# A hand-ordered attention and maxout-FFN kernel: a new order of the pieces behind the first 62, with its PSUM banks and drains, and four softmax products on VectorE

## The chip, the core and the metric

The kernel runs on one core of one Trainium2 chip, alone. The time is the device time of one execution in microseconds (us): the median of three executions of the kernel before is 164.94 us (164.56 to 165.78).

## What is computed

Eight batches of eight heads, 576 positions, head size 64. Each head's keys and values are first gathered into 32 memory slots with the softmax of `phi`; then every query attends to the 32 slots; the result goes through an FFN whose hidden layer is the largest of three products.

```python
a = softmax(phi, over positions)                    # (b, h, s, m), m = 32
k_m = einsum('bhsm,bhsd->bhmd', a, k)
v_m = einsum('bhsm,bhsd->bhmd', a, v)
attn = softmax(q @ k_m.T / 8, over the 32 slots)
x = (attn @ v_m) as (4608 tokens, 512)
h = maximum(maximum(x @ w1, x @ w2), x @ w3)        # 768 wide
out = h @ w_out                                     # 512 wide, float32
```

All inputs are float32 in HBM; the loads turn them into bfloat16 on the way (`phi` stays float32).

## The kernel before

The whole kernel is straight-line code. Every batch is cut into pieces, and one long list of words, written out by hand, says in which order the pieces are emitted: `F8@2` is piece F8 of batch 2. Each engine carries out its own instructions in the order in which they were emitted; across engines only semaphores hold them to data and to buffers. So the list is at once the order of TensorE (PE), of VectorE (DVE), of ScalarE (ACT), of GpSimd (POOL) and of POOL's loads.

The letters:

- `L0` to `L3` start a load on POOL's queue: phi, k, v and q of a batch, 576 KB each as it lands. `H`, `Y` are the loads of batch 0 and of the weights. A load has to wait, with POOL behind it, until the buffer that it fills has been read: phi and q have two buffers each, k and v of even and of odd batches one each (`kvo0`, `kvo1`).
- `E`: ACT takes the exponential of phi (L229). `r0`, `r1`: POOL packs k, then v, of a batch into one tile, `kvr` (L103). `B`: PE multiplies them, 72 small products (L249); it needs both packs. `N`: DVE normalises. `K`: PE transposes, a drain follows.
- `Q0`, `Q1`: DVE transposes the two halves of q (L313). `S`: PE's scores (L333), and ACT's exponential of them (L342).
- `a`, `s`, `c`, `m`, `X` with 0 or 1: the softmax over the 32 slots for one half of the heads: DVE transposes (L387), sums (L395), takes the reciprocal (L404); POOL multiplies (`m`, L409); DVE transposes back into `attn` (L417). There are 14 of each.
- `D0` to `D3`: the slots' values are folded into the weights (PE L440, then a drain to `wp`). `F0` to `F11`: the FFN's first layer for a batch, 4 matmuls each (L466). An even F is drained by a ReLU (L170 on ACT), an odd F by a maximum on DVE (L479), which writes `hT`.
- `T0` to `T4`: the second layer for 128 tokens: 6 matmuls with `wo_sb` and `hT` (L497), 2 with `wp3` and `attn` (L506; 4 at L515 for T4), a drain to `ot` (L172), and a store on SP's queue. `T` of a batch needs all its `hT`.

PSUM's eight banks are handed out by a second list, one digit a use; B, S, D and F take the bank named and the next one. A piece on PE waits until the last reader of its banks is done. Which of ACT and DVE drains a piece is in `EVAC`; a `!` behind a word turns it round for that piece:

```python
EVAC = {"D": "avaaa", "T": "vavav", "K": "v", "W": "vvv", "O": "aaaa", "F": "aaaaaa"}
if (EVAC[kind][n] == "a") != swap:
```

So T0, T2 and T4 are drained by DVE without a mark and by ACT with one; T1 and T3 the other way round.

Of the kernel before, what the change touches and what calls it, by code (L numbers as in the profile page):

```python
# [15 lines left out]
def kernel(  # L16
# [68 lines left out]
    def load_ph(b):  # L85
        ph = inp.tile([P, NP, NC, M], FP32, name="ph")
        loaded.setdefault(b, {})["ph"] = ph
        dst = ph.rearrange("p j c m -> p j (c m)")
        if b == 0:
            for h in halves:  # L90
                nc.sync.dma_start(out=dst[:, h], in_=by_pair(phi, b)[:, h])
        else:
# [8 lines left out]

    def pack(b, i):
        nc.gpsimd.tensor_copy(  # L103
            out=kvrs[b % 2][:, :, :, D * i : D * (i + 1)], in_=kvos[b % 2][:, 1 - i]
        )
# [132 lines left out]
    def att_kv(b, part=None):  # L238
        s = st[b]
        kvp = two_banks()  # L240
        s["kvp", part] = kvp
        kv = loaded[b]["kv"]
        nd = {None: 2 * D + 1, 0: 2 * D, 1: D}[part]
        kvr = kvrs[b % 2]
        for c in range(NC):
            for j in range(NP):
                for a in range(NG):
                    r = slice(HP * a, HP * (a + 1))
                    nc.tensor.matmul(  # L249
                        kvp[M * j : M * (j + 1), a, 0:nd],  # L250
                        lhsT=s["e"][r, j, c, :],
                        rhs={
                            None: lambda: kvr[r, j, c, 0:nd],
                            0: lambda: k_and_ones(kv, r, j, c),
                            1: lambda: kv[r, 0, j, c, :],
                        }[part](),
                        start=(c == 0),
                        stop=(c == NC - 1),
                        tile_position=(HP * a, M * j),
                    )  # L260
# [331 lines left out]


    for w in """
        E@0 H2@0 H0@0 L3@0 Z25@0 B0@0 Y2@0 I@0 N0@0 Z2@0 K0@0! Q0@0 Q1@0 Z9@0 S@0 Z2@0 M0@0 M1@0
        R0@0 R1@0 W0@0 Y3@0 W1@0 W2@0 Z6@0 O1@0 H3@0 O3@0 O2@0 H1@0 X1@0 B1@0 X0@0 N1@0
        K1@0 O0@0 Y0@0 D1@0! D0@0! D3@0 F8@0 F10@0 F2@0 V0@0 F6@0 F0@0! Y1@0 D2@0 D4@0 F4@0
        L0@1 V1@0 F1@0 E@1 F3@0 L1@1 F5@0 F9@0 F7@0 L3@1 F11@0 B0@1 T3@0 N0@1 K0@1! L2@1 Q1@1
        L2@2 L1@2 Q0@1 L0@2 V2@0 T0@0! L3@2 S@1 T1@0 a0@1 s0@1 c0@1 m0@1 B1@1 N1@1 a1@1 L1@3
        K1@1 s1@1 D0@1 D1@1! D2@1 c1@1 m1@1 X0@1 L3@3 r1@2 X1@1 T2@0! L2@3 F6@1 F10@1 F7@1 F2@1  # L600
        F3@1 F4@1 F0@1 r0@2 E@2 F5@1 F1@1 F11@1 L0@3 L0@4 F8@1 L2@4 F9@1 B@2 D3@1 N@2 Q1@2
        T0@1! K@2 T2@1! r0@3 Q0@2 S@2 a0@2 a1@2 s1@2 c1@2 m1@2 T4@1! D1@2! s0@2 D2@2 c0@2 m0@2
        X1@2 D0@2 T3@1 Q0@3 L3@4 X0@2 Q1@3 T1@1 F0@2 F4@2 F8@2 F6@2 F9@2 E@3 F7@2 r1@3 F5@2
        F10@2 F1@2 B@3 L1@4 D3@2 N@3 L0@5 F2@2 F11@2 E@4 F3@2 L1@5 K@3 r1@4 L2@5 T2@2! S@3 T3@2
        a0@3 s0@3 c0@3 m0@3 D0@3 D2@3 a1@3 s1@3 c1@3 X0@3 D1@3! Q0@4 m1@3 T1@2 L3@5 L2@6 T0@2!
        X1@3 F10@3 r0@4 F2@3 F4@3 E@5 Q1@4 r0@5 F5@3 F3@3 L1@6 F8@3 B@4 N@4 D3@3 F9@3 F6@3
        F11@3 L0@6 K@4 F0@3 F7@3 F1@3 S@4 a0@4 T4@3! s0@4 a1@4 D0@4 c0@4 s1@4 r1@5 c1@4 D3@4
        m0@4 X0@4 Q0@5 T0@3! D1@4! D2@4 B@5 T3@3 m1@4 X1@4 L0@7 F10@4 Q1@5 N@5 F8@4 K@5 F6@4
        F9@4 S@5 F7@4 L3@6 F2@4 F4@4 a0@5 L1@7 a1@5 F0@4 s0@5 r1@6 F3@4 D0@5 r0@6 s1@5 c1@5 E@6
        D3@5 m1@5 c0@5 F1@4 T1@3 L2@7 F11@4 L3@7 E@7 F5@4 m0@5 B@6 D1@5! D2@5 X1@5 N@6 T2@3!  # L610
        X0@5 F6@5 F8@5 Q0@6 Q1@6 K@6 F4@5 F9@5 S@6 F7@5 r0@7 a0@6 F2@5 a1@6 s0@6 c0@6 F0@5
        F10@5 m0@6 F1@5 s1@6 c1@6 F11@5 F5@5 T0@4! F3@5 X0@6 T2@4! r1@7 D0@6 D1@6! Q0@7 B@7
        m1@6 N@7 X1@6 T2@5! K@7 T3@4 Q1@7 S@7 a0@7 F2@6 s0@7 a1@7 s1@7 c1@7 m1@7 c0@7 F4@6
        T4@5! D3@6 D2@7 D0@7! T0@5! D3@7 D2@6 X1@7 m0@7 D1@7! T1@4 X0@7 F6@7 F3@6 T1@5 F4@7
        F8@7 F0@7 F5@6 F10@6 F7@7 F9@7 F10@7 F5@7 F0@6 F11@7 F6@6 F1@7 F7@6 F2@7 F8@6 F11@6
        F9@6 F1@6 F3@7 T0@6! T0@7! T3@5 T2@7! T2@6! T1@6 T1@7 T3@6 T4@7! T3@7
    """.split():
# [32 lines left out]
```

## Time and profile before

| | before |
|---|---|
| median of three executions (lowest to highest) | 164.94 us (164.56 to 165.78) |
| profiled execution: span from first to last instruction | 163.3 us |
| mean granted PE clock in it | 0.995 |
| POOL's load queue: packets, share of the 16 DMA engines' span | 16080, 68.7% |
| store queue of SP: packets, share | 5728, 17.2% |
| HBM read, written | 39.32 MB, 9.44 MB |
| PE waits in the profile from 46 to 115 us (over 0.15 us) | none |

The span is that of one execution under the profiler; the median is 1.6 us above it. A busy PE in the profile may still wait a little between matmuls, since their ends are modelled; its real pace is read from the starts of equal matmuls.

The trace also has the moment at which each load had landed. The loads behind the weights land one after the other in the order in which they were issued; k3 is the k of batch 3, ph4 the phi of batch 4:

| place | before: load | issued, us | landed, us |
|---|---|---|---|
| 1 to 4 | ph1, k1, q1, v1 | 9.4 to 19.9 | 32.2, 34.8, 37.7, 40.5 |
| 5 to 8 | v2, k2, ph2, q2 | 24.7 to 31.2 | 44.1, 48.5, 50.0, 53.5 |
| 9 to 11 | k3, q3, v3 | 43.5, 45.6, 48.4 | 56.3, 59.1, 63.5 |
| 12, 13 | ph3, ph4 | 51.2, 51.9 | 65.6, 67.2 |
| 14 | v4 | 52.7 | 71.3 |
| 15 | q4 | 62.3 | 74.2 |
| 16 to 19 | k4, ph5, k5, v5 | 65.6 to 73.4 | 77.3, 79.2, 83.0, 87.3 |
| 20 to 23 | q5, v6, k6, ph6 | 77.6 to 85.9 | 89.8, 94.0, 98.0, 100.1 |
| 24 to 28 | ph7, q6, k7, v7, q7 | 91.7 to 102.9 | 102.0, 104.7, 108.3, 111.8, 114.6 |

Stores of 256 KB run beside them: 18 land between 44.1 and 112.4 us.

### The profile page before, as it was taken

The page shows a single profiled execution, that of the slowest core. Times are in us where ns is not written, and L with a number is a line of the kernel's source. Part 1 is how long each engine was busy: PE and PEld are TensorE (multiplying, and loading weights), DVE is VectorE, ACT ScalarE, POOL GpSimd, SP SyncE. Part 2 cuts the span into 40 slices and gives each one's busy share as a digit, 9 for nine tenths or more (in the row PEclk, how much of TensorE's full clock was granted, in tenths as well). Part 3 has the DMA queues.
Part 4 walks back from the last instruction along what each step waited for, and adds up shares of the span by engine and source line. Part 5 has one row for each costly group of instructions (what it writes and reads, how often), then busy time and mean ns, then how long its engine had stood idle before and what let it go on. Part 6 is the DMA issues. An engine that isn't in the chain of part 4 may idle for free.

```text
span 163.3 us, 4838 instructions
## 1 busy us (share of the span) xinstructions
PE 153.8 (94%) x2080; PEld 85.3 (52%) x2080; DVE 90.4 (55%) x181; ACT 100.6 (62%) x151; POOL 69.5 (43%) x71
## 2 busy tenths in 40 slices
PE   7978798899899999999999999999999999999990
PEld 2433444564377436743673575576553468744450
DVE  2023704798838665849399748879749128810010
ACT  4205445845497488778885899994658976223320
POOL 7932205100599259657968957646403100000000
PEclk9999999999999999999999999999999999999998
DMA  6999999999999999999999999996313130014333
GB/s 150 152 206 207 205 210 217 274 208 210 253 313 238 209 253 379 274 210 293 252 263 206 232 355 264 191 233 150 130 69 129 69 128 0 0 68 186 135 128 130
DMA packets 21974, 31.77 MB, mean 195 GB/s; under 512 B 1216, under 2 KB 16576, under 8 KB 21952
## 3 DMA queue, kind: packets, MB, share of 16 engines
q0 software_dynamic: 16080, 21.43, 68.7%
q1 hardware_dynamic: 5728, 9.90, 17.2%
q8 instruction: 16, 0.26, 0.6%
q10 hardware_dynamic: 144, 0.13, 0.2%
q14 instruction: 6, 0.05, 0.1%
HBM read 39.32 MB, written 9.44 MB: 299 GB/s over the span
## 4 chain that ended last, share of the span: by engine, by line
PE 83%; DMA 9%; POOL 2%; ACT 2%; issue 1%; DVE 1%; ACTq 0%; POOLq 0%
PE psum L497 29%; PE psum L466 28%; DMA wo_sb<-in_moe_w_out_dram 9%; PE psum L506 8%; PE psum L440 6%; PE psum L249 4%; PE psum L192 3%; PE psum L333 2%; PE psum L515 1%; ACT h L170 1%; PE psum L538 1%; PE psum L298 1%; POOL kvo L97 1%; ACT wp L172 1%; POOL qq L110 0%
## 5 line engine op out<-in xcount | busy, mean ns | idle before, releaser
L497 PE MATMUL psum<-wo_sb,hT 128*128 128x512 bf16 x210 | 51.3, 380 | 0.0
L466 PE MATMUL psum<-attn,wp 128*128 128x288 bf16 x384 | 50.5, 286 | 0.1
L479 DVE TENSOR_TENSOR hT<-psum,h 128x576 bf16<-128x576 f32 x48 | 34.2, 749 | 18.0 <-PE psum L466 12.5
L466 PEld LDWEIGHTS <-wp 128*128 128x128 bf16 x384 | 36.7, 98 | 13.2 <-issue 2.0
L172 ACT COPY ot<-psum 128x512 f32<-128x512 f32 x35 | 20.7, 591 | 32.1 <-PE psum L506 25.2
L497 PEld LDWEIGHTS <-hT 128*128 128x128 bf16 x210 | 19.2, 97 | 24.0 <-issue 4.3
L172 ACT CAST wp<-psum 128x1024 bf16<-128x1024 f32 (+1 forms) x31 | 29.2, 995 | 3.8 <-PE psum L440 2.0
L103 POOL COPY kvr<-kvo 128x2304 bf16<-128x2304 bf16 x12 | 25.3, 2111 | 13.7 <-DMA kvo<-in_k_dram 10.1
L170 ACT ACTIVATE h<-psum 128x576 bf16<-128x576 f32 x47 | 28.4, 659 | 3.5 <-PE psum L466 3.3
L409 POOL TENSOR_TENSOR t<-t,sm 128x576 bf16<-128x576 bf16 x14 | 16.1, 1154 | 24.6 <-DVE sm L404 24.4
L506 PE MATMUL psum<-wp,attn 128*128 128x512 bf16 x62 | 18.4, 379 | 0.0
L159 PE MATMUL psum<-warm 128*128 128x512 bf16 x44 | 12.1, 427 | 1.2 <-DVE warm L128 1.2
L313 DVE STREAM_TRANSPOSE qT<-qq 128x576 f32<-128x576 f32 x16 | 11.7, 747 | 1.4 <-DMA qq<-in_q_dram 1.4
L342 ACT ACTIVATE e<-psum 128x576 bf16<-128x576 f32 x16 | 9.6, 652 | 3.8 <-PE psum L333 3.8
L229 ACT ACTIVATE e<-ph 128x1152 bf16<-128x1152 f32 (+1 forms) x9 | 9.6, 1065 | 1.7 <-DMA ph<-in_phi_dram 1.6
L395 DVE TENSOR_REDUCE sm<-t 128x18 f32<-128x576 bf16 x14 | 10.3, 738 | 0.2
L387 DVE STREAM_TRANSPOSE t<-e 128x288 f32<-128x288 f32 x14 | 6.4, 465 | 6.2 <-ACT e L342 6.1
L97 POOL DMA_DIRECT2D kvo<-in_v_dram x9 | 6.7, 749 | 7.1 <-PE psum L249 4.1
L506 PEld LDWEIGHTS <-attn 128*128 128x128 bf16 x62 | 6.1, 98 | 7.1
L110 POOL DMA_DIRECT2D qq<-in_q_dram x8 | 6.2, 770 | 6.6 <-DVE h L174 3.7
L555 DVE COPY ot<-psum 128x256 f32<-128x256 f32 x1 | 0.4, 425 | 15.4 <-PE psum L546 15.4
L249 PEld LDWEIGHTS <-e 64*32 64x32 bf16 x720 | 6.9, 90 | 3.7 <-issue 3.3
(57 smaller groups left out, 114.4 us busy)
## 6 DMA issues: line engine op xcount, KB each, us to landing
out_dram<-ot SPq DMA_DIRECT2D x35, 256.0 KB, 5.6
qq<-in_q_dram POOLq DMA_DIRECT2D x8, 576.0 KB, 12.2
ph<-in_phi_dram POOLq DMA_DIRECT2D x7, 576.0 KB, 14.4
kvo<-in_k_dram POOLq DMA_DIRECT2D x7, 576.0 KB, 14.6
kvo<-in_v_dram POOLq DMA_DIRECT2D x7, 576.0 KB, 15.6
w_sb<-in_moe_w_dram POOLq DMA_DIRECT2D x3, 768.0 KB, 19.0
wo_sb<-in_moe_w_out_dram POOLq DMA_DIRECT2D x1, 768.0 KB, 14.6
ph<-in_phi_dram SPq DMA_DIRECT2D x2, 288.0 KB, 3.0
```

Of the source, the lines that this page charges most:

```text
L103: nc.gpsimd.tensor_copy(out=kvrs[b % 2][:, :, :, D * i : D * (i + 1)], in_=kvos[b % 2][:, 1 - i])
L159: nc.tensor.matmul(po[:, 0:BANK], lhsT=warm[:, 0:P], rhs=warm, start=True, stop=True)
L170: nc.scalar.activation(out=out_, in_=in_, func=AF.Relu)
L172: nc.scalar.copy(out=out_, in_=in_)
L249: nc.tensor.matmul(kvp[M * j : M * (j + 1), a, 0:nd], lhsT=s["e"][r, j, c, :], rhs={None: lambda: kvr[r, j, c, 0:nd], 0: lambda: k_and_one ...
L313: nc.vector.transpose(out=s["qT"][:, j].rearrange("p j c r e -> p (j c r e)").bitcast(FP32), in_=loaded[b]["q"][:, j].rearrange("p j c d - ...
L395: nc.vector.tensor_reduce(out=sm, in_=s["t", g].rearrange("p n r e -> p n e r"), op=ALU.add, axis=mybir.AxisListType.X,)
L409: nc.gpsimd.tensor_tensor(out=t, in0=t, in1=s["sm", g].unsqueeze(2).to_broadcast([P, S // HP, R, 2]), op=ALU.mult,)
L466: nc.tensor.matmul(acc[:, h, 0:SH], lhsT=wps[b][:, g, w * DF + ft * P : w * DF + (ft + 1) * P], rhs=attn[:, g, c0 : c0 + SH], start=(g == ...
L479: nc.vector.tensor_tensor(out=hT[:, ft, (b % 2) * S : (b % 2 + 1) * S].rearrange("p (h n) -> p h n", h=2), in0=a, in1=s["h1", ft], op=ALU.max,
L497: nc.tensor.matmul(po, lhsT=hT[:, fc, c0 : c0 + P], rhs=wo_sb[:, fc, :], start=(n == 0), stop=False,)
L506: nc.tensor.matmul(po, lhsT=attn[:, g, c0 : c0 + P], rhs=wp3s[b][:, g, :], start=False, stop=(g == NG - 1),)
```

## The change

The first 62 words of the order stay as they are. Behind them all words are the same in kind and number, 368 in all, and stand in another order; the bank list is new from its fourth digit on; the marks `!` sit on other words (33 before, 42 after). `m` takes a mark now, and four have one: `m1@1`, `m1@2`, `m0@2` and `m0@5` run on DVE. `r` could take one (ACT would pack), and none has it.

By kind, the drains that change hands: six ReLUs of F (128x576) go from ACT to DVE, twelve drains of T (128x512) and three of D (128x1024) go from ACT to DVE, and four drains of K (128x384) go from DVE to ACT.

```diff
-    def pack(b, i):
-        nc.gpsimd.tensor_copy(
-            out=kvrs[b % 2][:, :, :, D * i : D * (i + 1)], in_=kvos[b % 2][:, 1 - i]
-        )
+    def pack(b, i, swap):
+        out_, in_ = kvrs[b % 2][:, :, :, D * i : D * (i + 1)], kvos[b % 2][:, 1 - i]
+        if swap:
+            nc.scalar.copy(out=out_, in_=in_)
+        else:
+            nc.gpsimd.tensor_copy(out=out_, in_=in_)
...
-            00224460026701101401264026402640264026452063420643064206420642064562074206742064
...
+            00232204420145545045024602460460246024674620540246206246024604260160272046740624
...
-    def att_mul(b, g):
+    def att_mul(b, g, swap):
         s = st[b]
         t = s["t", g]
-        nc.gpsimd.tensor_tensor(
+        (nc.vector if swap else nc.gpsimd).tensor_tensor(
...
-        L0@1 V1@0 F1@0 E@1 F3@0 L1@1 F5@0 F9@0 F7@0 L3@1 F11@0 B0@1 T3@0 N0@1 K0@1! L2@1 Q1@1
-        L2@2 L1@2 Q0@1 L0@2 V2@0 T0@0! L3@2 S@1 T1@0 a0@1 s0@1 c0@1 m0@1 B1@1 N1@1 a1@1 L1@3
-        K1@1 s1@1 D0@1 D1@1! D2@1 c1@1 m1@1 X0@1 L3@3 r1@2 X1@1 T2@0! L2@3 F6@1 F10@1 F7@1 F2@1
-        F3@1 F4@1 F0@1 r0@2 E@2 F5@1 F1@1 F11@1 L0@3 L0@4 F8@1 L2@4 F9@1 B@2 D3@1 N@2 Q1@2
-        T0@1! K@2 T2@1! r0@3 Q0@2 S@2 a0@2 a1@2 s1@2 c1@2 m1@2 T4@1! D1@2! s0@2 D2@2 c0@2 m0@2
-        X1@2 D0@2 T3@1 Q0@3 L3@4 X0@2 Q1@3 T1@1 F0@2 F4@2 F8@2 F6@2 F9@2 E@3 F7@2 r1@3 F5@2
-        F10@2 F1@2 B@3 L1@4 D3@2 N@3 L0@5 F2@2 F11@2 E@4 F3@2 L1@5 K@3 r1@4 L2@5 T2@2! S@3 T3@2
-        a0@3 s0@3 c0@3 m0@3 D0@3 D2@3 a1@3 s1@3 c1@3 X0@3 D1@3! Q0@4 m1@3 T1@2 L3@5 L2@6 T0@2!
-        X1@3 F10@3 r0@4 F2@3 F4@3 E@5 Q1@4 r0@5 F5@3 F3@3 L1@6 F8@3 B@4 N@4 D3@3 F9@3 F6@3
...
+        D2@0 D4@0 F4@0 L0@1 V1@0 F1@0 E@1 F3@0 L1@1 F5@0 F9@0 F7@0 L3@1 F11@0 B0@1 N0@1
+        Q0@1 Q1@1 V2@0 T3@0 K0@1! T0@0 S@1 L2@1 a0@1 B1@1 L0@2 s0@1 N1@1 c0@1 T1@0 L1@2
+        L2@2 a1@1 K1@1 D0@1 s1@1 c1@1 m0@1 X0@1 m1@1! D1@1! X1@1 D2@1! T2@0! F0@1 F6@1!
+        L0@3 F2@1 F10@1! L3@2 F3@1 r0@2 E@2 F8@1 F7@1 F11@1 F4@1 F1@1 F9@1 L2@3 F5@1
+        D3@1 r1@2 B@2 E@3 N@2 T0@1! K@2! Q0@2 Q1@2 T2@1 S@2 T1@1 D1@2! D0@2 a0@2 D3@2
+        L1@3 a1@2 s0@2 T3@1 T4@1! L2@4 L3@3 s1@2 c1@2 r1@3 L0@4 D2@2 m1@2! X1@2 r0@3
+        c0@2 B@3 L1@4 m0@2! L1@5 X0@2 N@3 L3@4 F0@2 r1@4 F4@2 F8@2 F2@2 L0@5 L2@5 r0@4
+        Q0@3 Q1@3 F5@2 F1@2 L1@6 F6@2 E@4 F3@2 F9@2 F10@2 L3@5 F7@2 F11@2 K@3 T2@2 S@3
+        a0@3 B@4 s0@3 D3@3 c0@3 m0@3 a1@3 T1@2 s1@3 N@4 c1@3 X0@3 T3@2 m1@3 D1@3 X1@3
+        D0@3 Q1@4 D2@3 L0@6 T0@2! F6@3 Q0@4 F4@3 r0@5 F8@3 F5@3 E@5 L2@6 F9@3 F2@3 F7@3
...
```

The banks of the pieces that the prediction walks through, in the new list: B@3 0, F0@2 6, F4@2 2, F8@2 4, F2@2 6, F5@2 0, F1@2 2, F6@2 4, F3@2 6, F9@2 0, F10@2 4, F7@2 2, F11@2 6.

More of the change, by code (lines that the diff above doesn't have):

```diff
@@ L140 @@
             """
-            00224460026701101401264026402640264026452063420643064206420642064562074206742064
-            20642064201640264102640264026402640264072406247026402640264024602406520462046204
-            62704267402640264124602416420642064206420642067676767670
+            00232204420145545045024602460460246024674620540246206246024604260160272046740624
+            60246042601624067042602604260426042604267260430626024062402602640246240264034602
+            42046201624042614620460426426420640460424026062467676764
             """.split()
@@ L569, in issue @@
             "H": lambda: load_kv(b, i % 2, halves[i // 2]),
-            "r": lambda: pack(b, i),
+            "r": lambda: pack(b, i, swap),
             "E": lambda: [att_exp(b, h) for h in (halves if b == 0 else [slice(0, NP)])],
@@ L579, in issue @@
             "c": lambda: att_rec(b, i),
-            "m": lambda: att_mul(b, i),
+            "m": lambda: att_mul(b, i, swap),
             "X": lambda: (ones_mul if (b, i) in ONES else att_back)(b, i),
@@ L594 @@
     for w in """
-        E@0 H2@0 H0@0 L3@0 Z25@0 B0@0 Y2@0 I@0 N0@0 Z2@0 K0@0! Q0@0 Q1@0 Z9@0 S@0 Z2@0 M0@0 M1@0
-        R0@0 R1@0 W0@0 Y3@0 W1@0 W2@0 Z6@0 O1@0 H3@0 O3@0 O2@0 H1@0 X1@0 B1@0 X0@0 N1@0
-        K1@0 O0@0 Y0@0 D1@0! D0@0! D3@0 F8@0 F10@0 F2@0 V0@0 F6@0 F0@0! Y1@0 D2@0 D4@0 F4@0
-        L0@1 V1@0 F1@0 E@1 F3@0 L1@1 F5@0 F9@0 F7@0 L3@1 F11@0 B0@1 T3@0 N0@1 K0@1! L2@1 Q1@1
-        L2@2 L1@2 Q0@1 L0@2 V2@0 T0@0! L3@2 S@1 T1@0 a0@1 s0@1 c0@1 m0@1 B1@1 N1@1 a1@1 L1@3
-        K1@1 s1@1 D0@1 D1@1! D2@1 c1@1 m1@1 X0@1 L3@3 r1@2 X1@1 T2@0! L2@3 F6@1 F10@1 F7@1 F2@1
@@ L607 @@
[L607 to L616, printed above, removed]
+        E@0 H2@0 H0@0 L3@0 Z25@0 B0@0 Y2@0 I@0 N0@0 Z2@0 K0@0! Q0@0 Q1@0 Z9@0 S@0 Z2@0
+        M0@0 M1@0 R0@0 R1@0 W0@0 Y3@0 W1@0 W2@0 Z6@0 O1@0 H3@0 O3@0 O2@0 H1@0 X1@0 B1@0
@@ new lines @@
+        X0@0 N1@0 K1@0 O0@0 Y0@0 D1@0! D0@0! D3@0 F8@0 F10@0 F2@0 V0@0 F6@0 F0@0! Y1@0
+        D2@0 D4@0 F4@0 L0@1 V1@0 F1@0 E@1 F3@0 L1@1 F5@0 F9@0 F7@0 L3@1 F11@0 B0@1 N0@1
[3 more added lines that the diff above has]
+        D3@1 r1@2 B@2 E@3 N@2 T0@1! K@2! Q0@2 Q1@2 T2@1 S@2 T1@1 D1@2! D0@2 a0@2 D3@2
@@ new lines @@
+        L1@3 a1@2 s0@2 T3@1 T4@1! L2@4 L3@3 s1@2 c1@2 r1@3 L0@4 D2@2 m1@2! X1@2 r0@3
[3 more added lines that the diff above has]
+        D0@3 Q1@4 D2@3 L0@6 T0@2! F6@3 Q0@4 F4@3 r0@5 F8@3 F5@3 E@5 L2@6 F9@3 F2@3 F7@3
+        F10@3 r1@5 F3@3 K@4! F0@3 L3@6 F11@3 S@4 F1@3 B@5 a0@4 N@5 D2@4 L1@7 D3@4 s0@4
@@ new lines @@
+        c0@4 T3@3 K@5! Q1@5 a1@4 s1@4 c1@4 T1@3! m0@4 D0@4 D1@4! Q0@5 m1@4 X0@4 X1@4
+        D2@5 T4@3 S@5 a0@5 L0@7 a1@5 r1@6 T2@3! s0@5 F6@4! F2@4 F0@4 F4@4 s1@5 F1@4 F3@4
+        F10@4 L2@7 F7@4 F8@4 L3@7 F11@4 c0@5 r0@6 c1@5 E@6 F9@4 T0@3! F5@4 m1@5 D1@5!
+        D0@5 B@6 m0@5! X1@5 X0@5 N@6 Q0@6 T3@4 F4@5 F10@5! F0@5 F11@5 F8@5 K@6 r0@7 Q1@6
+        F9@5 F5@5 F1@5 T0@4 E@7 r1@7 S@6 B@7 D3@5 a0@6 T2@4! a1@6 N@7 Q0@7 F6@5 F2@5!
+        D1@6! D3@6 F3@5 Q1@7 s1@6 c1@6 K@7! T1@4 F7@5 s0@6 S@7 c0@6 T3@5! D2@7! a1@7
@@ L617 @@
+        a0@7 m1@6 m0@6 X0@6 s0@7 c0@7 X1@6 m0@7 D2@6 D0@6 T4@5! D3@7 D1@7 D0@7 s1@7 c1@7
+        T0@5! F10@6 F2@6 F3@6 X0@7 m1@7 F6@6 X1@7 F11@6 F4@6 T1@5 F0@6 F10@7 F4@7! F1@6
+        F8@6 F7@6 F11@7 T2@5! F2@7 F5@6 F9@6 F8@7 T3@6 F3@7 F0@7 F5@7 F9@7 T1@6! F6@7
+        F1@7 F7@7 T2@6 T0@7 T4@7! T1@7! T2@7! T0@6 T3@7
     """.split():
```

## The prediction

> **What bounds the kernel now.** I first read the page's busy times and slices, then the busy time by stage.
>
> ```profile
> PE 153.8 (94%) x2080; PEld 85.3 (52%) x2080; DVE 90.4 (55%) x181; ACT 100.6 (62%) x151; POOL 69.5 (43%) x71
> ...
> DMA  6999999999999999999999999996313130014333
> ```
>
> ```profile
> core 0: us, PE busy (x) PEld busy (x) DVE busy (x) ACT busy (x) POOL busy (x), PEclk, DMA share, GB/s
> ...
> 46.00:68.00 22.00, 22.00 (x300) 13.31 (x299) 14.24 (x28) 17.39 (x26) 15.77 (x14) 1.00 1.15 277
> 68.00:115.00 47.00, 46.98 (x766) 27.48 (x743) 36.26 (x78) 37.51 (x54) 33.25 (x28) 1.00 1.11 239
> ```
>
> PE has no idle time from 46 to 115 us, so there a new order can win hardly anything. The second thing to see is that the loads are just as full: the DMA digits are 9 up to 110 us, and by the table of landings one load ends as the next begins, from 26 to 114.6 us. The n-th load lands at a time set by the loads ahead of it, whenever it was issued. So there are two clocks, PE's work and the queue of loads, and the old order fits them together. The question is whether the new one still does. POOL's timeline and the chain of waits show the fit:
>
> ```profile
> 56.34 2.11 POOL L103 COPY kvr<-kvo 128x2304 bf16<-128x2304 bf16 x1 [2.90 <-DMA kvo<-in_k_dram]
> ...
> 63.51 2.11 POOL L103 COPY kvr<-kvo 128x2304 bf16<-128x2304 bf16 x1 [0.39 <-DMA kvo<-in_v_dram]
> ...
> 71.38 2.11 POOL L103 COPY kvr<-kvo 128x2304 bf16<-128x2304 bf16 x1 [2.30 <-DMA kvo<-in_v_dram]
> ```
>
> ```profile
> 63.39 4.41 PE psum L466 x36
> 67.80 0.73 PE psum L249 x68
> ...
> 77.11 1.29 PE psum L497 x6
> 78.41 0.43 PE psum L506 x2
> ...
> 81.78 0.73 PE psum L249 x71
> ```
>
> POOL packs as soon as k or v is there (56.3, 63.5, 71.4 us), so it is already waiting for loads; PE runs B@3 at 67.80, 2.2 us after its last pack, and B@4 at 81.78. The chain gives the prices: an F 4.41/9 = 0.49, B 0.73, a T 1.29 + 0.43 = 1.73.
>
> **The order of PE against the loads.** I count pieces. The old order has PE at 67.80 when it begins B@3. In the new order the work ahead of F9@2 is the same set with B@3, D3@2 (0.22), F2@2 and F3@2 more and F10, F7 and F9@2 less: 0.73 + 0.22 + 0.98 - 1.47 = +0.46. Unhindered, PE comes to F9@2 at 68.26. B@4 follows after F9, F10, F7, F11 (1.96), K@3 (0.17), T2@2 (1.73) and S@3 (0.42), at 72.5. In the old order twelve further pieces, 8.8 us of them (three T, three D, six F), stood ahead of B@4. So the new order wants batch 4 nine us earlier, and the loads cannot give it.
>
> Landing of q3. In the new order the loads behind the weights are ph1 k1 q1 v1, ph2 k2 v2, ph3 q2 v3 k3, v4 q3 ph4, k4. The first fourteen are the same fourteen loads as in the old order, where the last of them landed at 71.3 (the third POOL row). ph4 is now last and takes 67.2 - 65.6 = 1.6; q3, the thirteenth, lands at 69.6. In the old order it landed at 59.1. The store traffic can shift this: ph4, the old thirteenth, landed at 67.2, and v4 in its place costs 1.2 more (2.8 for a lone k, v or q), so 68.4 is the early end.
>
> Who waits. Q0@3 and Q1@3 stand on DVE ahead of the maximum of F5@2, and a DVE that waits for q3 lets nothing pass. DVE has finished N@3 by about 66.3 (B@3 at 64.5, then 0.73 and 1.05 of L269 to L283). So it stands idle until 69.65, transposes twice (0.74 each, 0.70 apart), and ends the maximum of F5@2 (0.75) at 71.80. PE meanwhile gets through F1, F6 and F3 (their banks come free from ACT or earlier work), but F9@2 takes bank 0, F5's. It starts at 71.86: 3.60 late.
>
> Landing of k4. It is fifteenth, and the first fifteen are again the same set, whose last landed at 74.2. POOL's pack takes 2.11, so B@4 starts at 74.2 + 0.05 + 2.11 + 0.06 = 76.4 at the earliest: 3.9 late against 72.5. From F9's late start B@4 would come at 71.86 + 4.28 = 76.1, so this second bound adds only 0.3: the two overlap. Third, B@3: k3 lands eleventh, at 63.5 less 1.2 (ph3 stands in q3's place) = 62.3; packed at 64.4; wanted at 67.80 - 4.41 + 0.22 = 63.6, so 0.8 late, inside the 3.9 because the later landings do not move with it. v5, place 19, lands at 87.3 and v6, place 23, at 100.1, as before; B@5 and B@6 then want 89.5 and 102.4 and come, 3.9 late, at 90.9 and 108.8. The delay is paid once: **3.9 us**.
>
> **What else moves.** The ahead-of-68 part (new bank list, D and T earlier, K0@1 behind T3@0) can lose or win only what the wall at 71.9 and 76.4 absorbs: nothing up to about 3.9 us of loss, and a win there only lengthens the wait. The old idle of PE between 20 and 46 (26.0 - 24.2 = 1.8 us) is therefore no gain.
>
> VectorE's products: no row shows one. Nearest is the product of 128x576 in SBUF at L377, 0.75 us; bounds 0.47 (L417, half the elements as float32) and 1.15 (the same product on POOL). I take 0.75: 4 x 0.75 = 3.0 us onto DVE, 4 x 1.15 = 4.6 off POOL. Two of them (m1@2, m0@2) lie just ahead of N@3 on DVE, which waits 3 us for q3 behind them; POOL's relief serves packs that wait for loads. I count nothing; without that cover the bounds are 1.9 to 4.6 us.
>
> Drains: DVE gets 6 x 0.76 (L174) + 12 x about 0.70 (between 0.43 for 256 columns and 1.23 for 1024) + 3 x 1.23 - 4 x 0.34 = 15.3, with the products 18.3, to 109 us; ACT loses 6 x 0.66 + 12 x 0.59 + 3 x 1.0 - 4 x about 0.45 = 12.2. Neither fills its span. Zero, with a bound of 2 us for the stretch from 115 to 135, where many of them lie.
>
> After the wall PE's order is looser. At the paces of the chain's rows the old PE work from 68 to 159.6 needs 89.6 of 91.6 us; 2.0 us are small waits inside busy time. I take 0.3 of it back, between 0 and 1.9.
>
> Sum: 163.3 + 3.9 - 0.3 = 166.9 of span; the median stands 1.6 above the span, so **168.5 us**.
>
> **Rivals.**
>
> *The clock falls in the wait.* Between F3@2 and F9@2 PE is idle for up to 3.4 us. At the end of the old run the granted clock is 0.50 from 161.7, 2.1 us after the last matmul's end (159.58); at its start matmuls run at half pace for 3.5 us, 9 against 18 in windows of the same length (columns: window, length, PE busy and matmuls, granted clock, DMA; the first grant on record is at 4.7):
>
> ```profile
> 1.20:4.70 3.50, 3.50 (x9) 1.00 0.81 189
> 4.70:8.20 3.50, 3.50 (x18) 1.00 1.11 166
> ...
> 161.70:163.30 1.60, 0.00 (x0) 0.50 0.01 5
> ```
>
> Half pace for 3.5 us from 71.86 loses 1.75, of which the 0.3 to B@4's bound was waiting anyway: 1.5 more, 170.0. Against it: the 0.8 at B@3 shortens the idle to 2.8, and the fall was seen once, where no matmul was left to come. By these rows it is open; I give it 0.28. [...]
>
> *The wall is thinner.* Loads land earlier, for stores that no longer fall among them: with q3 at 67.2 and k4 at 72 the delay is under 1.7, 165 to 166. For it: the store rows' share (17%) is movable. Against: the same nine stores precede. 0.09.
>
> *Faster.* If q3 were down by 65.9 and k4 by 70.3 (some four us under the counts above), PE would never stop; the looser order then wins the 2.0 us of small waits: 161.3 + 1.6 = 163.0. It decides at a delay under 0.4. Nothing in the landings supports it. 0.05.
>
> *DVE becomes the bound* behind B@7, where both halves of batch 6's softmax now stand (2 x 1.94 from L387, L395, L404 and L417) beside more drains: 2 us on top of the wall, 170.5. Against it: DVE was busy for only half of the time from 115 to 135. 0.06.
>
> **How the numbers follow.** The forecast has 0.52. About 1%, 1.65 us, is what a measurement of this kernel can tell from no change. Slower by more: forecast, clock and DVE, 0.52 + 0.28 + 0.06 = 0.86; same 0.09; faster 0.05. Range: low from both landings 1.2 earlier (delay 2.7) with 0.9 recovered, 164.9 + 1.8 = 166.7; high from the clock rival with landings 0.5 later, 170.5.
>
> **What would show it.** A DVE wait of 3 to 4 us ahead of a pair of L315 transposes at about 69.6, ended by the landing of q; PE idle before an L468 matmul until about 72; POOL's pack of k at about 74.2. Wrong if PE has no wait over 1 us after 60; if q3 lands before 67; if the waits sit before T drains instead; and the clock rival is right if matmuls behind 72 are spaced at twice their pace.

## The result, and the profile after

The changed kernel takes 170.66 us (169.74 to 171.63, four executions) against 164.91 us (164.56 to 165.78) for the kernel before on the same chip: ratio 1.033, 95% interval 1.028 to 1.038. A second set gave 169.88 us (169.26 to 170.40) against 165.00, ratio 1.027 (1.022 to 1.032). The forecast was 168.5, its range 166.7 to 170.5; the first median lies 0.16 above the range, the second inside it. Ratios leave out executions over 1.5% above the fastest of the same kernel; where an experiment has such, all its times are told.

| | before | after |
|---|---|---|
| profiled execution: span | 163.3 us | 168.0 us (its time 169.74) |
| mean granted PE clock in it | 0.995 | 0.987 |
| DVE busy | 90.4 us | 108.8 us |
| ACT busy | 100.6 us | 91.1 us |
| landed: k3, q3, ph4, k4 | 56.3, 59.1, 67.2, 77.3 us | 61.2, 69.7, 71.3, 74.0 us |

The page of the changed kernel, its busy times and two rows of slices:

```profile
PE 154.2 (92%) x2061; PEld 86.5 (51%) x2080; DVE 108.8 (65%) x202; ACT 91.1 (54%) x134; POOL 65.3 (39%) x67
...
PE   7986799999999999389999999999999999999991
...
PEclk9999999999999999959999999999999999999998
```

There is one hole in PE's row, in slices 17 and 18 (67 to 76 us), and the second of these has about half the clock. The rest of the row is as full as before. The timeline of the changed kernel shows what the hole consists of (start, length, engine, line; in brackets the idle time before it and who ended it):

```profile
64.67 4.09 PE L468 MATMUL psum<-attn,wp 128*128 128x288 bf16 x32
...
69.69 1.44 DVE L315 STREAM_TRANSPOSE qT<-qq 128x576 f32<-128x576 f32 x2 [3.94 <-DMA qq<-in_q_dram]
71.05 2.71 DVE L481 TENSOR_TENSOR hT<-psum,h 128x576 bf16<-128x576 f32 x4
...
71.82 3.57 PE L468 MATMUL psum<-attn,wp 128*128 128x288 bf16 x16 [3.05 <-DVE hT L481]
...
74.06 2.11 POOL L107 COPY kvr<-kvo 128x2304 bf16<-128x2304 bf16 x1 [4.80 <-DMA kvo<-in_k_dram]
...
77.63 0.80 PE L251 MATMUL psum<-kvr,e 64*32 64x129 bf16 x72
```

VectorE stands for 3.94 us until q3 has landed, transposes it, and only then takes the maximum of F5@2 whose bank F9@2 needs. F9@2 starts at 71.82. Its 16 matmuls (F9, F10, F7 and F11) then take 3.57 us where the same 16 take 2.12 us in an execution whose clock holds (the first experiment). The same place cut into stretches of 3.41 us (columns: window, length, PE, weight loads, DVE, ACT and POOL busy with the number of instructions, granted clock, DMA share, GB/s):

```profile
64.57:67.98 3.41, 3.36 (x33) 2.66 (x28) 1.03 (x5) 2.93 (x5) 3.37 (x4) 1.00 1.15 280
67.98:71.39 3.41, 0.79 (x7) 0.49 (x5) 1.70 (x3) 0.68 (x2) 1.28 (x2) 1.00 1.13 298
71.39:74.81 3.42, 2.99 (x13) 1.92 (x13) 2.37 (x4) 1.78 (x2) 0.75 (x1) 0.50 1.21 207
```

PE is busy for 0.79 us of the second stretch, and the whole third stretch has half the clock. So of the 4.7 us by which the span is longer, the wait is 3.05 and the half pace 3.57 - 2.12 = 1.45, together 4.5.

### The profile page after: what moved, and what is told of

Read it like the earlier page. It is cut to its first block, busy times and chain, and to the rows that moved or that the text cites. A ratio compares the mean times of both kernels' runs of the same rounds, so it can differ in the third digit from the quotient of the medians.

```text
span 168.0 us, 4821 instructions
## 1 busy us (share of the span) xinstructions
PE 154.2 (92%) x2061; PEld 86.5 (51%) x2080; DVE 108.8 (65%) x202; ACT 91.1 (54%) x134; POOL 65.3 (39%) x67
## 4 chain that ended last, share of the span: by engine, by line
PE 56%; DMA 32%; POOL 4%; DVE 3%; issue 2%; ACT 0%; DVEq 0%; POOLq 0%
PE psum L468 20%; PE psum L499 20%; DMA kvo<-in_v_dram 13%; DMA qq<-in_q_dram 10%; DMA wo_sb<-in_moe_w_out_dram 9%; PE psum L508 6%; PE psum L194 3%; PE psum L442 3%; PE psum L251 2%; POOL kvo L97 2%; POOL kvr L107 1%; PE psum L335 1%; PE psum L517 1%; DVE t L411 1%; DVE hT L481 1%
## 5 line engine op out<-in xcount | busy, mean ns | idle before, releaser
L468 PE MATMUL psum<-attn,wp 128*128 128x288 bf16 x384 | 52.0, 291 | 3.3 <-DVE hT L481 3.1
L499 PE MATMUL psum<-wo_sb,hT 128*128 128x512 bf16 x195 | 49.4, 380 | 1.4 <-issue 0.8
L468 PEld LDWEIGHTS <-wp 128*128 128x128 bf16 x384 | 37.6, 99 | 17.6 <-issue 4.9
L172 ACT ACTIVATE h<-psum 128x576 bf16<-128x576 f32 x41 | 25.4, 654 | 11.1 <-PE psum L468 11.0
L174 ACT CAST wp<-psum 128x1024 bf16<-128x1024 f32 (+1 forms) x28 | 26.5, 989 | 4.9 <-PE psum L442 4.9
L411 POOL TENSOR_TENSOR t<-t,sm 128x576 bf16<-128x576 bf16 x10 | 11.5, 1154 | 44.1 <-DVE sm L406 44.1
L174 ACT COPY ot<-psum 128x512 f32<-128x512 f32 x23 | 13.5, 588 | 25.5 <-PE psum L508 17.2
L178 DVE COPY ot<-psum 128x512 f32<-128x512 f32 x12 | 8.3, 690 | 10.8 <-PE psum L508 6.5
L161 PE MATMUL psum<-warm 128*128 128x512 bf16 x42 | 12.5, 455 | 1.4 <-DVE warm L130 1.2
L161 PEld LDWEIGHTS <-warm 128*128 128x128 bf16 x44 | 4.6, 113 | 7.5 <-issue 3.7
L442 PE MATMUL psum<-w_sb,kvt 64*32 64x512 bf16 (+1 forms) x200 | 7.8, 372 | 0.6 <-DVE kvt L178 0.3
```

Of the source, the lines that this page charges most:

```text
L161: nc.tensor.matmul(po[:, 0:BANK], lhsT=warm[:, 0:P], rhs=warm, start=True, stop=True)
L172: nc.scalar.activation(out=out_, in_=in_, func=AF.Relu)
L174: nc.scalar.copy(out=out_, in_=in_)
L411: (nc.vector if swap else nc.gpsimd).tensor_tensor(out=t, in0=t, in1=s["sm", g].unsqueeze(2).to_broadcast([P, S // HP, R, 2]), op=ALU.mult,)
L442: nc.tensor.matmul(ps[M * j : M * (j + 1), a, 0 : hi - lo], lhsT=lhs[r, M * j : M * (j + 1)], rhs=rhs[r, j, :], start=(i == 0), stop=(i == ...
L468: nc.tensor.matmul(acc[:, h, 0:SH], lhsT=wps[b][:, g, w * DF + ft * P : w * DF + (ft + 1) * P], rhs=attn[:, g, c0 : c0 + SH], start=(g == ...
```

## The experiments

The runs were made in four sets, each on one chip beside its own runs of the kernel before (medians 165.22, 165.00, 165.25 and 164.98 us). "Excess" is the median above that of the kernel before in the same set. One figure helps to read them: in the traces of the changed kernel (both of them), e2 and e3, 86.65 to 86.67 us pass from the start of B@4 to the end of the last matmul. So in these runs the time is set by when B@4 starts, which is 77.63 us in the profile above.

| run | median (lowest to highest), us | ratio (95%) | excess, us |
|---|---|---|---|
| e1 ten idle matmuls ahead of F9@2 | 169.61 (168.85 to 169.74) | 1.022 (1.016 to 1.029) | 4.4 |
| e2 without the load of v4 | 166.26 (165.64 to 167.48) | 1.006 (1.002 to 1.009) | 1.0 |
| e3 q3 and ph4 used later | 170.72 (169.02 to 171.70) | 1.027 (1.019 to 1.035) | 5.5 |
| e4 products back on GpSimd | 168.49 (168.40 to 169.29) | 1.018 (1.013 to 1.024) | 3.3 |
| e5 the changed kernel again | 169.88 (169.26 to 170.40) | 1.027 (1.022 to 1.032) | 4.9 |
| e6 repaired order | 168.43 (167.77 to 168.56) | 1.019 (1.015 to 1.023) | 3.4 |
| e7 old order, q3 behind v4 | 176.50 (175.89 to 176.99) | 1.068 (1.064 to 1.073) | 11.5 |
| e8 old order, four products on DVE | 170.28 (166.54 to 171.26) | 1.010 (1.007 to 1.014), lower three | 5.3 (lower three 1.7) |
| e11 repaired order, products on GpSimd | 169.69 (168.55 to 171.32) | 1.029 (1.021 to 1.037) | 4.4 |
| e12 old order, three products on DVE | 166.80 (166.19 to 167.33) | 1.010 (1.007 to 1.013) | 1.8 |

### e1: does the clock fall because PE is idle?

Ten matmuls of the kernel's own warming kind (L161) go ahead of F9@2, into a bank that is free there; nothing reads what they write.

```diff
-        Q0@3 Q1@3 F5@2 F1@2 L1@6 F6@2 E@4 F3@2 F9@2 F10@2 L3@5 F7@2 F11@2 K@3 T2@2 S@3
+        Q0@3 Q1@3 F5@2 F1@2 L1@6 F6@2 E@4 F3@2 Z10@2 F9@2 F10@2 L3@5 F7@2 F11@2 K@3 T2@2 S@3
```

> The changed kernel with ten matmuls on zeros (2.15 us at full pace) put between F3@2 and F9@2, into a bank that is free there. Theory (wait plus fall of the clock): the wait for q3 stays, F9@2 still starts at 71.8, but PE's longest idle stretch there is about 1 us, the granted clock stays 1.00 from 65 to 76, the matmuls behind 72 run at 0.12 us apart instead of 0.24, and B@4 comes at 76.4 instead of 77.6; 169.4 us, 1.2 under the changed kernel. Rival (the slow stretch behind 72 is the drains of F on DVE, 0.70 each, and not the clock): the matmuls stay as far apart and the time stays at 170.5 to 170.9.

Its timeline:

```profile
69.03 2.32 PE L161 MATMUL psum<-warm 128*128 128x512 bf16 x9 [0.31 <-ACT h L172]
72.34 2.12 PE L468 MATMUL psum<-attn,wp 128*128 128x288 bf16 x16 [0.99 <-DVE hT L481]
...
74.23 2.11 POOL L107 COPY kvr<-kvo 128x2304 bf16<-128x2304 bf16 x1 [4.93 <-DMA kvo<-in_k_dram]
...
76.83 0.80 PE L251 MATMUL psum<-kvr,e 64*32 64x129 bf16 x72
...
78.25 0.39 PE L442 MATMUL psum<-w3o,kvt 64*32 64x512 bf16 x2 [0.40 <-issue]
```

The wait for q3 is still there and PE is kept busy in it; the granted clock stays at 1.00, and the 16 matmuls take 2.12 us again. q3 landed 0.5 us later than in the changed kernel's trace, so F9@2 starts at 72.34. B@4 starts at 76.83 instead of 77.63; k4 is packed by then (at 76.34), and PE simply arrives no earlier. In this execution those 0.8 us are lost again at once. Between the sixth and the seventh of the eight matmuls of D3@3 PE stands, 0.79 us from start to start, for nothing that the profile shows, and B@5 starts at 91.30, as in the changed kernel (91.31). The time is 169.6, 0.3 to 1.1 below the changed kernel in its two sets, and the intervals overlap. That the idle PE brings the clock down is shown by the clock and the pace: behind the stretch with PE busy for 0.79 of 3.41 us the changed kernel has 0.50 and 3.57 us for the 16 matmuls, and with PE kept busy there it is 1.00 and 2.12. What the clock is worth in whole time this run doesn't show. The kernels that took both clocks, e3 and e11, show it better.

### e2: are the late loads the wall?

L2@4 is left out: the v of batch 4 is not loaded, and B@4 reads the v of batch 2 in its place.

```diff
-        L1@3 a1@2 s0@2 T3@1 T4@1! L2@4 L3@3 s1@2 c1@2 r1@3 L0@4 D2@2 m1@2! X1@2 r0@3
+        L1@3 a1@2 s0@2 T3@1 T4@1! L3@3 s1@2 c1@2 r1@3 L0@4 D2@2 m1@2! X1@2 r0@3
```

> The changed kernel without the load of v of batch 4 (its product then reads the v of batch 2). Theory (the place in the load queue): q3 and k4 land one load earlier, 2.8 to 4.4 us, at about 66 and 70.5; DVE's wait for q3 falls from 3.9 to under 1 us, B@4 comes at 72.7 to 73.5 instead of 77.6, no fall of the clock; 165.5 to 166.5 us, and 1.0 to 1.5 over the kernel before at most. Rival (the new order or its heavier DVE is slow in itself): PE still loses 3 us or more behind 60, and the time stays above 168.

Three lines of its timeline:

```profile
64.61 6.05 PE L468 MATMUL psum<-attn,wp 128*128 128x288 bf16 x48 [0.19 <-DVE attn L419]
...
65.62 1.44 DVE L315 STREAM_TRANSPOSE qT<-qq 128x576 f32<-128x576 f32 x2
...
73.52 0.80 PE L251 MATMUL psum<-kvr,e 64*32 64x129 bf16 x72 [0.53 <-POOL kvr L107]
```

With one load less ahead of them, q3 lands at 65.6 (4.1 earlier) and k4 at 71.3. The twelve F of batch 2 run through in 6.05 us, B@4 waits 0.53, and 166.26 us are left: as forecast in the expectation. All but 1 us of the loss hangs on the queue of loads. How much of that is the two landings alone this run can't tell, since every later load moves up as well: v5 lands at 83.96 instead of 85.94, and e6 shows that it is the next one to be waited for. And even so the new order isn't faster than the old.

### e3: the second wall by itself

Q0@3 and Q1@3 move behind K@3, E@4 behind S@3, so that nothing waits for q3 and ph4; k4 stays where it was.

```diff
-        Q0@3 Q1@3 F5@2 F1@2 L1@6 F6@2 E@4 F3@2 F9@2 F10@2 L3@5 F7@2 F11@2 K@3 T2@2 S@3
-        a0@3 B@4
+        F5@2 F1@2 L1@6 F6@2 F3@2 F9@2 F10@2 L3@5 F7@2 F11@2 K@3 Q0@3 Q1@3 T2@2 S@3 E@4
+        a0@3 B@4
```

> The changed kernel with Q0@3 and Q1@3 moved behind K@3 and E@4 behind S@3, so that no drain of F@2 stands behind a wait for q3 or ph4. Theory (a second wall right behind the first): F@2 runs through, and B@4 waits for k4 and its pack instead, with PE idle 2.2 to 2.8 us before it, at 76.2 to 76.4; 168.7 us if the clock holds, 170 if it falls again. Rival (the wait for q3 is the whole loss): B@4 by 73.5 and 165 to 166.5 us.

The timeline of its profiled execution, the pack of k4 and B@4:

```profile
74.70 2.11 POOL L107 COPY kvr<-kvo 128x2304 bf16<-128x2304 bf16 x1 [4.92 <-DMA kvo<-in_k_dram]
...
76.87 0.80 PE L251 MATMUL psum<-kvr,e 64*32 64x129 bf16 x72 [2.40 <-POOL kvr L107]
```

The wait for q3 is gone and the next one takes its place: k4 lands at 74.7, is packed, and B@4 starts at 76.87, as late as in e1. The rival's 165 to 166.5 us falls. The profiled execution took 169.02 us at full clock. Two took 170.54 and 170.90 with a mean granted clock of 0.99, and one 171.70 with 0.98; one stretch of 3.41 us at half clock takes 0.01 off the mean, and two take 0.02. One kernel thus has both: the clock falls in some of its executions, and those with one such stretch are 1.5 to 1.9 us longer.

### e4: the products alone

The four marks at `m` go; everything else of the change stays.

```diff
-        c1@1 m0@1 X0@1 m1@1! D1@1!
+        c1@1 m0@1 X0@1 m1@1 D1@1!
...
```

> The changed kernel with all 14 products on GpSimd, in the same order. Theory (what happens ahead of the wall is absorbed by it): q3 and k4 land as before within 0.5 us, so the time stays within 1.0 us of 170.7. Rival (the products on VectorE are what costs, for they hold it or wait for GpSimd's packs): 1.5 us or more faster. Second rival (they win by taking GpSimd out of the way): 1.5 us or more slower.

Its timeline from m0@2 to F9@2:

```profile
65.10 1.17 POOL L411 TENSOR_TENSOR t<-t,sm 128x576 bf16<-128x576 bf16 x1
...
66.70 0.13 DVE L271 RECIPROCAL rden<-psum 128x2 f32<-128x2 f32 x1
66.84 4.09 PE L468 MATMUL psum<-attn,wp 128*128 128x288 bf16 x32 [1.64 <-DVE rden L271]
...
72.07 2.12 PE L468 MATMUL psum<-attn,wp 128*128 128x288 bf16 x16 [1.15 <-DVE hT L481]
```

The expectation (within 1.0 us of 170.7) missed: the kernel is 2.2 us faster than the changed one in its first set, 1.4 than in the second. On GpSimd m0@2 has to stand behind the pack of k3 and the issue of the load of k4, and VectorE, which transposes its result back, comes to N@3 2 us later (66.70 against 64.74). PE pays for that with 1.64 us ahead of F0@2. But F9@2 starts at 72.07, as before: q3 decides that. What was one wait of 3.05 us is now two, of 1.64 and 1.15, in two stretches of which PE is busy for 52% and 73%, and the clock holds at 1.00. So the rival's number came, but not by its cause: on VectorE the products did bring PE forward, into a wait that was there anyway, and made it one of 3.05 us, with a clock of 0.50 behind it.

### e5: the changed kernel again

> The changed kernel once more, as the base of this set. Theory (two late loads and a clock that falls in the wait for the first): 170 to 171.5 where the clock falls, at about 71.4 for 3.4 us; near 169 in a run where it holds. Rival (the fall is an accident of one execution): 168.5 to 169.

Of its timeline the line behind the wait:

```profile
72.50 3.53 PE L468 MATMUL psum<-attn,wp 128*128 128x288 bf16 x16 [3.44 <-DVE hT L481]
```

In this execution the wait is 3.44 us and the 16 matmuls behind it take 3.53; the clock has 0.5 from 72.00 to 75.41. All four executions, like the four of the first set, have a mean clock of 0.980 to 0.990, as one or two such stretches make it. The fall is no accident of one.

### e6: a repair of the order around the wall

The 36 words between r0@4 and T0@2! stand in another order (the expectation names 28, up to D3@3), with banks to suit; the order of the loads and the engines of the products stay. T1@2 and T3@2, which stood behind D3@3, are now ahead of B@4.

```diff
-        Q0@3 Q1@3 F5@2 F1@2 L1@6 F6@2 E@4 F3@2 F9@2 F10@2 L3@5 F7@2 F11@2 K@3 T2@2 S@3
-        a0@3 B@4 s0@3 D3@3
+        F5@2 F1@2 F3@2 F6@2 F9@2 F7@2 F10@2 F11@2 K@3 Q0@3 T2@2 E@4 T1@2 Q1@3 S@3 a0@3
+        T3@2 B@4 a1@3 L1@6 L3@5 D3@3
...
```

> The changed kernel with 28 words between r0@4 and D3@3 in another order: all of F of batch 2 first, then K@3, Q0@3, T2@2, E@4, T1@2, Q1@3, S@3, T3@2, B@4. Loads and products stay. Theory: q3 (lands 69.7) is now wanted by S@3 at 68.3 + 1.96 + 0.17 + 3.46 = 73.8 and needs 69.7 + 1.5 + 0.1 = 71.3, and k4 by B@4 at 73.8 + 0.42 + 1.73 = 76.0 with 76.4 possible, so no wait over 0.5 us ahead of B@4 and no fall of the clock: as without the load of v4, 166.3, bounds 165.3 and 167.5. Rival (the drains or VectorE's load cost the time, and the late loads only show it): above 168.5.

PE's waits in its timeline:

```profile
64.86 6.19 PE L468 MATMUL psum<-attn,wp 128*128 128x288 bf16 x48 [0.22 <-DVE attn L419]
...
79.00 0.41 PE L442 MATMUL psum<-w_sb,kvt 64*32 64x512 bf16 x8 [1.10 <-ACT wp L174]
...
89.79 0.80 PE L251 MATMUL psum<-kvr,e 64*32 64x129 bf16 x72 [0.75 <-POOL kvr L107]
```

Up to B@4 the theory holds: F runs through, B@4 starts at 76.87 without a wait that the profile shows, and the clock is 1.00 throughout. But the time is 168.43, not the 166.3 expected. It lies just under the rival's 168.5, and the two waits behind B@4 tell why. PE waits 1.10 us in the D pieces of batch 3, since ScalarE is still draining D3@3 (to 78.94). In the changed kernel T1@2 and T3@2 stood between these pieces; this edit moved them away, so this wait comes from the edit. And PE waits 0.75 us at B@5, whose v5 landed only at 87.6. Without the two it would be about 166.6, an estimate. The two named waits for the loads and the clock are repaired; the queue of loads is still behind the order.

### e7: the place of one load, in the old order

```diff
-        K1@1 s1@1 D0@1 D1@1! D2@1 c1@1 m1@1 X0@1 L3@3 r1@2 X1@1 T2@0! L2@3 F6@1 F10@1 F7@1 F2@1
-        F3@1 F4@1 F0@1 r0@2 E@2 F5@1 F1@1 F11@1 L0@3 L0@4 F8@1 L2@4 F9@1
+        K1@1 s1@1 D0@1 D1@1! D2@1 c1@1 m1@1 X0@1 r1@2 X1@1 T2@0! L2@3 F6@1 F10@1 F7@1 F2@1
+        F3@1 F4@1 F0@1 r0@2 E@2 F5@1 F1@1 F11@1 L0@3 L0@4 F8@1 L2@4 L3@3 F9@1
```

> The kernel before with one word moved: the load of q3 behind that of v4. Theory (a load's place sets its landing, and a VectorE that waits for it stops every drain behind it): q3 lands at 69.5 instead of 59.1; VectorE, which in the old order has Q0@3 ahead of the maxima of batch 2, stands until then, and PE stops at the first F that needs a bank of these; PE is 7 to 9 us late and the clock falls in the wait: 172 to 175. Rival (it is the new order of PE and the drains that costs the time, not the place of a load): 165 to 166.

Its timeline, VectorE and PE at the wait:

```profile
71.09 0.78 DVE L313 STREAM_TRANSPOSE qT<-qq 128x576 f32<-128x576 f32 x1 [9.37 <-DMA qq<-in_q_dram]
71.79 0.44 DVE L417 STREAM_TRANSPOSE attn<-t 128x288 f32<-128x288 f32 x1
...
72.28 6.64 PE L466 MATMUL psum<-attn,wp 128*128 128x288 bf16 x36 [8.93 <-DVE attn L417]
```

One moved load makes the old kernel 11.5 us slower. VectorE waits 9.37 us for q3, `attn` of batch 2 is queued behind that, and PE stands for 8.93, from F0@2 on. The expectation had it stop a little later, at an F that needs a bank, and its 172 to 175 us were too low. q3 landed at 71.07; the 69.5 of the expectation was miscounted, since here it is the fourteenth load, and the fourteenth of the kernel before landed at 71.3. The clock has 0.5 for 10.24 us; the nine F after the wait take 6.64 us against 4.57 in the kernel before. Wait and half pace, 8.93 and 2.07, make 11.0 of the 11.9 us between the spans (175.2 and 163.3).

### e8 to e10, and e12: the products in the old order

```diff
-        K1@1 s1@1 D0@1 D1@1! D2@1 c1@1 m1@1 X0@1
+        K1@1 s1@1 D0@1 D1@1! D2@1 c1@1 m1@1! X0@1
...
```

Likewise m1@2, m0@2 and m0@5 in e8 to e10; e12 leaves m1@1 on GpSimd.

> The kernel before with only the four products m1@1, m1@2, m0@2 and m0@5 on VectorE. Theory (a product of 0.75 us, up to 1.9 beside a pack, in an order where VectorE has spare time): within 1 us of the kernel before, 164.5 to 166. Rival (the products themselves cost PE's time, a term that the prediction put at nothing): 166.5 or more.

> The old order with four products on VectorE, once more, for its profile: of seven executions three took 166.5 to 167.1 and four 170.3 to 171.3. Theory (the clock, as in the changed kernel): an execution of about 170 shows a record of half pace of 3.4 us and a wait on PE ahead of it. Rival (a load that slips a place): one or more loads behind the eighth land 2 us or more later than in the kernel before, at full clock. In an execution of about 166.7 neither.

> The same kernel a second time, since which of its two times an execution takes is not the choice of whoever runs it: as for the look before.

> The old order with three products on VectorE; m1@1 back on GpSimd. Theory (a product on VectorE that meets a pack on GpSimd ends 0.6 us after the pack; m1@1 is the one that meets it in some executions, 3.41 us in place of 0.76, and the delay pushes m0@2 under the next pack): no execution at 170, all between 165.5 and 167.2, and no product of over 1 us in the profile. Rival (the two times come from elsewhere): some executions at 170 or more.

e8 gave two times: three executions of 166.54 to 167.13 us, four of 170.28 to 171.26. Both lie above the expected 164.5 to 166, as the rival had it. The profile of e8 is one of the lower; those of e9 and e10 are of the upper (171.31 and 170.24). The difference begins at m1@1. The timeline of e8 there:

```profile
44.23 0.75 POOL L112 DMA_DIRECT2D qq<-in_q_dram  x1
44.29 0.76 DVE L411 TENSOR_TENSOR t<-t,sm 128x576 bf16<-128x576 bf16 x1
44.96 2.12 POOL L107 COPY kvr<-kvo 128x2304 bf16<-128x2304 bf16 x1
```

The timeline of e9:

```profile
45.22 3.41 DVE L411 TENSOR_TENSOR t<-t,sm 128x576 bf16<-128x576 bf16 x1
45.88 2.12 POOL L107 COPY kvr<-kvo 128x2304 bf16<-128x2304 bf16 x1
49.07 6.17 PE L468 MATMUL psum<-attn,wp 128*128 128x288 bf16 x48 [2.12 <-DVE attn L419]
...
62.75 2.11 POOL L107 COPY kvr<-kvo 128x2304 bf16<-128x2304 bf16 x1 [2.25 <-DMA kvo<-in_v_dram]
63.45 2.02 DVE L411 TENSOR_TENSOR t<-t,sm 128x576 bf16<-128x576 bf16 x1
...
68.68 1.51 PE L468 MATMUL psum<-attn,wp 128*128 128x288 bf16 x11 [1.90 <-DVE attn L419]
```

In both the product begins 0.66 to 0.67 us ahead of a pack on GpSimd. In e8 it is done in 0.76 us; in e9 it takes 3.41 and ends 0.62 us after the pack. Everything behind it is pushed back, so that m1@2 comes to lie under the next pack (2.02 us). PE waits 2.12 and 1.90 us for `attn`, where e8 has 0.63 at the second place and nothing at the first: 3.4 of the 4.5 us between the two spans (169.5 and 165.0). Of the expectation's two answers neither was right. The clock is 1.00 in e9 (0.995 in e10), two of the four upper executions of e8 have a mean of 1.00 as well and two one of 0.99, and no load up to the twenty-fifth lands 2 us later than in e8. e10 repeats it: 3.41 us at m1@1. With m1@1 back on GpSimd (e12) none of six executions is above 167.33, and the longest of the three products takes 0.759 us, as was expected.

The lower time has a cost too, 1.7 us. On GpSimd the two products of batch 2 (2.27 us from 60.10) ran beside VectorE's sums; on VectorE they stand in line with them. `attn` is complete at 64.03 instead of 62.89, and PE waits 0.63 ahead of F0@2 in e8, then 0.42 at 107.46, behind m0@5 (0.62 and 0.42 in e12). B@3 starts 0.86 us later than in the kernel before, B@5 1.05, B@7 1.64, and the last matmul ends 1.64 later.

### e11: the repaired order with the products on GpSimd

> The repaired order (all F of batch 2 first, then K@3, Q0@3, T2@2, E@4 and so on) with the four products on GpSimd again. Theory (in this order the products only matter through the clock, which does not fall here): 168.4, within 0.5 of the repaired order with the products on VectorE. Rival (the products cost PE's time as they do in the old order, 0.8 us ahead of F0@2 and about 0.6 near 105 us): 167.0.

The median, 169.69, is above both answers. Two executions (168.55, 168.92) have a clock of 1.00, two (170.46, 171.32) one of 0.99. The profiled one, 168.55, shows PE waiting 1.66 us ahead of F0@2, as in e4. Where the clock holds, the products' place is worth about 0.1 us in this order (168.43 in e6); why it falls in two executions was not seen, since no trace of these was taken. So at full clock the products gained nothing on VectorE in the two orders that show it: about nothing here, and 1.7 us lost in the old one.

## Why the prediction was right, and where it was not

**The two clocks.** Right. By the place in the queue of loads q3 was to land at 69.6 and k4 at 74.2: 69.7 and 74.0. F9@2 was to start at 71.86: 71.82. The wait is VectorE's, for q3, ahead of the maximum of F5@2, as described; e2 (one load less), e3 (the second wall alone) and e7 (one load moved) show that the landings cause it. PE came to F9@2 at 71.82 - 3.05 = 68.77 instead of 68.26, so the wait is 3.05 us and not 3.60. k3 landed 1.1 us earlier than counted, and B@3 started at 63.79, 0.2 late instead of 0.8. One waiter wasn't named: ScalarE stands 2.33 us for ph4 ahead of E@4; behind it, at 74.00, it waits for PE again, so nothing is late by that.

**The clock.** This step failed. The forecast held the clock up, because the fall was on record only once, with no matmul left to come, and the wait might be as short as 2.8 us; the fall had a chance of 0.28. It fell in all eight executions of the changed kernel: in both that were traced, and by the mean clock (0.980 to 0.990) in the other six. So the sum lacks this term; without the half pace the profiled span would be about 166.6 us, against the 166.9 of the sum. The rival had the term, and its 170.0 lies between the two medians (170.66 and 169.88). Its size, 1.5, is met in part by luck. It was made up of 1.75 of lost pace less 0.3 that k4's bound would take. Measured are 1.45, since F9@2 starts 0.43 us after the clock falls, and the bound takes next to nothing: without the half pace B@4 would start at 76.18, and k4 allows 76.23. The trace of before had the answer at its end: the fall at 161.70 came 2.1 us after the last matmul. That row was read as open and should have been the likelier. The kernel before isn't free of the fall either: one of its 40 executions in the four sets (166.41 us) has a mean clock of 0.99; it was not traced.

**The products.** Counted at nothing, with 0.75 us each and a bound of 1.15. In this order nothing is what they cost directly: the four take 0.71, 0.76, 1.89 and 1.65 us; VectorE waits for q3 soon behind the third, and PE shows no wait over 0.16 us behind B@4, so the fourth is covered too. But the bounds were too narrow (3.41 was measured in e9), and the cover is a matter of order: in the old one the same four cost 1.7 us or, in the upper executions (median 171.0), 6.0. And they have an indirect price here, the clock, which e4 shows.

**Drains.** VectorE was to reach 109 us and has 108.8. ScalarE lost 9.5 us, not 12.2. The stretch from 115 to 160 us, where VectorE was feared as a bound, has PE busy for 44.5 of 45 us. That rival fell.

**Thinner wall, and faster.** The first fell with the landings. The second is answered by e2: with the wait all but gone the new order takes 166.3 us, not 163.0. The 2.0 us of small waits that a looser order might win aren't seen as won.

## What to carry to other kernels

Where loads run without a gap, count the place of each load in the queue, read its landing from the load that had this place, and look which engine waits for it and what is queued behind that engine: one load four places later cost 11.5 us here (e7). A wait of 3.05 us on TensorE cost the clock on top here (0.50 for 3.41 us in the changed kernel), and two waits of 1.64 and 1.15 us did not (1.00 in e4). A product that moved to VectorE was priced here by what GpSimd did at that moment too, not by its own duration alone: m1@1 took 0.76 us in e8 and 3.41 in e9, where it ended 0.62 us after a pack.

## What the hardware did that was not expected

**The clock's records came in stretches of 3.41 us.** The records of the clock in the traces of before, after and e7 have lengths that are whole multiples of 3.413 us, the last record of a trace aside: 64.85, 3.41 and 92.16 us in the changed kernel are 19, 1 and 27 of them, 157.01 us in the kernel before are 46, and the half clock of e7, from 66.31 to 76.55 us, is 3. Where the grid of these stretches lies differs from execution to execution: the first rise to 1.0 is recorded at 4.69 us in the kernel before and at 6.54 in the changed one. PE's share of one stretch stands against the granted clock of the next:

| kernel | stretch, us | PE busy | clock in the next |
|---|---|---|---|
| e7 | 62.89 to 66.31 | 0.13 | 0.5 |
| e5 | 68.58 to 72.00 | 0.14 | 0.5 |
| after | 163.55 to 166.97 | 0.21 | 0.5 |
| after | 67.98 to 71.39 | 0.23 | 0.5 |
| e7 | 69.72 to 73.13 | 0.25 | 0.5 |
| before | 158.29 to 161.70 | 0.38 | 0.5 |
| e10 | 64.46 to 67.87 | 0.45 | 1.0 |
| e4 | 65.03 to 68.44 | 0.52 | 1.0 |
| e3 | 72.10 to 75.52, 75.52 to 78.93 | 0.56, 0.56 | 1.0 |

In these rows the clock of the next stretch is half after 0.38 or less and full after 0.45 or more. What lies between was not met. In the traces of before and after every other stretch between the first rise and the last matmul has PE busy for 0.61 or more, and the clock of the next is 1.0. The first rise is another matter. In the changed kernel PE is busy for 1.93 us (0.57) of the stretch that ends at 3.12 us, and in the next, up to 6.54, the warming matmuls still start 0.43 us apart; behind 6.54 they start 0.22 apart. So 0.57 was followed by half pace there, and 0.56 in e3 by the full clock.

These rows would explain why e3 has both kinds of execution, as an estimate: its 2.40 us of waiting were cut in two by the grid in the profiled one (0.56 and 0.56). That they were not in the other three is inferred from their mean clocks, not seen. The fall came behind stretches in which PE was not idle throughout, with a share of 0.25 in e7 and even of 0.38 in the kernel before, and the wait of 3.05 us in the changed kernel, shorter than the stretch of 3.41, did not keep the clock up.

**Products on VectorE that met a pack on GpSimd ended behind it.** Such products ended 0.61 to 0.62 us after the pack (they took 2.02 us in e9, 1.89 and 1.65 in the changed kernel, 3.41 at the worst, in e9); alone they take 0.71 to 0.76. It goes the other way too: packs that are recorded as starting under a running product take 2.24 us (from 61.25) and 2.46 (from 110.73) in the changed kernel, instead of 2.11, and end 1.96 to 1.97 us after the product. The recorded starts do not tell whether a product is held up: in e9 that of the product of 3.41 us lies 0.66 us ahead of the pack's, and in e8 0.67 us ahead, where the product was done in 0.76. What decides between the two, and by what the two engines hold each other up, the traces do not show; both have a load being issued on GpSimd at the same moment (0.75 us, from 44.23 in e8 and from 45.15 in e9).
